# A channel attention with a rational feed-forward: second product with stationary weights, half of it in float32r

## The chip, the cores and the metric

The kernel runs on one core of a Trainium2 chip. Its time is the device time of one execution in microseconds (us). Five engines work side by side, each through its own list of instructions in order: TensorE (PE) for matrix products, with its weight loads shown apart (PEld), VectorE (DVE), ScalarE (ACT), GpSimd (POOL), and SyncE (SP), which issues the DMAs.

## The reference

```
B, N, C = 4, 6080, 256;  F = 2048
qn = q / (norm(q, axis=1) + 1e-6);  kn = k / (norm(k, axis=1) + 1e-6)
a  = softmax(kn^T @ qn / tau)            # 256 x 256 per batch
x  = (v @ a) as 24320 x 256
h  = x @ w_in                            # 24320 x 2048
P  = a0 + a1 h + a2 h^2 + a3 h^3
Q  = 1 + |b0| |h| + |b1| h^2
g  = P / (Q + 1e-6)
out = g @ w_out                          # 24320 x 256
```

All in float32. The attention is small; the two products with w_in and w_out and the rational function between them, on 24320 x 2048 elements, are nearly all the work.

## The kernel before

The attention matrix of a batch is multiplied into w_in once ("fuse"), so that h of a batch is v times a fused 256 x 2048 weight. These weights and v are each split into a high part in float32r and a low rest in float32r.

Work goes in groups of 512 tokens, twelve to a batch, 48 in all; the last group of each batch has 448. A group is worked on in eight **pairs**; a pair is two blocks of 128 columns of h (`pair`, line 612). For one pair:

- `mm1` (625): the first product. For each of the two blocks six matmuls with 512 columns (high by high, high by low, low by high, for two blocks of 128 input channels) into `hx`, two PSUM banks.
- The denominator: in the plain form ScalarE squares h, GpSimd multiplies and adds one ("line"), ScalarE takes b0|h|, GpSimd adds ("sum", a two-tensor operation). In the factored form (|h| (b1|h| + b0)), for the pairs in `FACTORED` = 1, 3, 6 of all groups but the first, ScalarE, VectorE ("prod"), ScalarE make it, and GpSimd only adds one ("one").
- The numerator: ScalarE ("slope") and two operations of VectorE ("num1", "num2"), in place in `hx`.
- The quotient: ScalarE takes the reciprocal square root of the denominator and squares it ("root", "square": r), GpSimd multiplies the denominator by r ("again": d r, close to 1), VectorE multiplies the numerator by r ("quot"), and then by 2 - d r ("last", a Newton step), into `g`. All these work on both blocks at once, 128 x 1024 elements.
- `mm2` (679): the second product in float32. A block of g of 128 tokens is the stationary side and 256 columns of w_out move; four tokens blocks for each of two column blocks, summed over all pairs into `acc`, two PSUM banks.

PSUM has eight banks: three `hx` of two banks, one `acc` of two. After its eight pairs, `finish` (691) copies `acc` with ScalarE into `orow` and SyncE stores it. The v of the next group comes through `values` (586): eight turns on TensorE, a copy on ScalarE, a subtraction on VectorE ("vlo").

The order of all instructions is written out beforehand by a planner (`Planner`, 68). Every step has an engine, a cost, a key and the buffers that it reads and writes. The planner plays the engines forward with these costs; an engine that is free takes the ready step with the lowest key whose buffers are free. Keys are the pair's place in the sequence plus an offset by kind of step (`LAG`, `TIME`, 21 to 30). The order found is then issued as it is: each engine keeps to it. A buffer's slot is given back when its last reader is done.

The first 120 us hold the attention of batch 0, and the preparation of w_in and w_out (`piece`, 304), which arrive as 64-bit floats and are turned into float32 by six operations a piece, mostly on VectorE. The attention of the next batches is worked on beside the pairs.

Of the kernel before, what the change touches and what calls it, by code (L numbers as in the profile page):

```python
# [21 lines left out]
    "first": 1.66, "prod": -1.1, "abs": -4.14, "line": 6.02, "second": 2.32, "sum": -18.3, "slope": 3.87,  # L22
    "num1": 23.26, "num2": 17.29, "root": 6.75, "one": -11.27, "square": -9.08, "again": 5.6, "quot": 15.77,
    "last": 10.51, "out": 27.17,
}
TIME = {
    "pair": 4.08, "start": 48.71, "load": 1.95, "softmax": 50.67, "in": 4.96, "late_in": 4.46, "out0": 2.34,
    "out": 5.84, "attn0_0": -0.36, "attn_0": 0.78, "attn0": 3.79, "attn": 2.32, "attn1": 91.81,
    "value": 3.37, "fuse": 1.73, "finish": 7.89, "front": 48.7, "front_pace": 3.02,
}  # L30

# [18 lines left out]
class Buf:  # L50


    def __init__(self, tag=None, view=None):
        self.tag, self.view = tag, view
        self.tile, self.slot = None, None
        self.writers, self.readers = [], []
        self.left = 0
        self.owner, self.until = None, 0.0
# [4 lines left out]

class Step:
    __slots__ = ("eng", "cost", "fn", "key", "need", "after", "new", "bufs", "banks", "port", "n")


class Planner:
# [3 lines left out]

    HOP = {"PE": 0.25, "ACT": 0.07, "DVE": 0.07, "POOL": 0.07, "SP": 3.5}

    def __init__(self, slots, fifo, banks):
        self.slots, self.fifo, self.banks = slots, fifo, banks
        self.steps = []

    def add(self, eng, cost, key, fn, reads=(), writes=(), port=False):
        s = Step()  # L80
        s.eng, s.cost, s.fn, s.key = eng, cost, fn, key
        s.n = len(self.steps)
        s.port = port or eng == "POOL"
        s.after, s.new, s.bufs = [], [], []
        before = {}
        for b in reads:
            for w in b.writers:
                before[w.n] = w
            assert b.writers
# [21 lines left out]
    def order(self):  # L111
# [5 lines left out]
        for q in queue.values():  # L117
            q.sort(key=lambda s: (s.key, s.n), reverse=True)
# [9 lines left out]
        left = len(self.steps)  # L128

        def fits(s):  # L130
            want = {}
            for b in s.new:
                want[b.tag] = want.get(b.tag, 0) + 1
                if b.tag in queue and queue[b.tag][-1] is not s:
                    return False
            if any(b.owner != s.eng and b.until > now for b in s.banks):
                return False
            return all(len(free[t]) >= n for t, n in want.items())

        while left:  # L140
            for e in ready:
                while busy[e] <= now and ready[e]:
                    skipped, pick = [], None
                    while ready[e]:
                        entry = heapq.heappop(ready[e])
# [8 lines left out]
                    for b in pick.new:  # L154
                        b.slot = free[b.tag].pop(0)
                        if b.tag in queue:
                            queue[b.tag].pop()
                    out.append((now, pick))
                    left -= 1
                    busy[e] = now + pick.cost  # L160
                    if pick.port:
                        other = "POOL" if e == "DVE" else "DVE"
                        busy[e] = max(now, port[other]) + pick.cost
                        port[e] = busy[e]
                    for b in pick.banks:
                        b.owner, b.until = e, busy[e] + self.HOP[e]
                    heapq.heappush(events, (busy[e], 0, pick.n, pick))
                    heapq.heappush(events, (busy[e] + self.HOP[e], 1, pick.n, pick))
# [4 lines left out]
            while events and events[0][0] <= now:  # L173
                _, what, _, s = heapq.heappop(events)
                if what == 2:
# [16 lines left out]
def tile_channel_attention_rational_ffn(  # L192
# [25 lines left out]
    while n0 < N:  # L218
# [8 lines left out]
    FACTORED = (1, 3, 6)  # L227

# [10 lines left out]
    SLOTS = {"hx": 3, "acc": 1, "d": 4, "uu": 4, "r": 3, "g": 4, "w": 10, "kq": 4, "sq": 2, "ssq": 1,  # L239
             "vst": 1, "vhi": 2, "vlo": 2, "orow": 2, "sacc": 1, "eT": 1, "cv": 1, "cv2": 1, "n2": 1,  # L240
             "s0": 1, "y": 1, "e": 1, "rn": 1, "diag": 1, "row": 1, "ex": 2, "sm": 2, "st": 1}
    plan = Planner(SLOTS, ("d", "uu", "r", "g", "w", "kq", "sq", "cv", "cv2", "vst", "vhi", "vlo", "orow", "acc"), ("hx", "acc"))

# [22 lines left out]
    def step(eng, cost, key, fn, reads=(), writes=(), port=False):  # L266
        new = [b for b in writes if b.tag is not None and not b.writers]
# [6 lines left out]
        plan.add(eng, cost, key, run, reads, writes, port)  # L274
# [20 lines left out]
    w_out_sb = const.tile([P, NF, C], F32, name="w_out_sb")  # L295
# [8 lines left out]
    def piece(side, m, at, c):  # L304
# [9 lines left out]
        raw = buf("d" if early else "g", [P, 2 * PIECE], U32, "raw")  # L314
        kept = buf("uu" if early else "cv", [P, 2, PIECE], F32, "kept")
        work = buf(("acc" if side == "in" and m < 4 else "hx") if early else "cv2", [P, 2, PIECE], F32, "work")
# [39 lines left out]
        def cut_off():  # L356
# [3 lines left out]
                dst, keep(), 1.125 * 2.0**-15, unit(F32), op0=ALU.is_ge, op1=ALU.mult  # L360
            )

        if side == "in":
            dst, ok = w_in_sb[:, j, cols], w_in_ok[part, j]
        else:
            dst, ok = w_out_sb[:, 2 * m : 2 * m + 2].rearrange("p f e -> p (f e)"), w_out_ok[m]
# [8 lines left out]
        step("DVE", two, c + 0.5, cut_off, [work, kept], [ok], port)  # L375


    class Attn:
# [3 lines left out]
        def __init__(self, b, begin, pace, end, gate=()):  # L382
# [3 lines left out]
            sps = buf("hx", [P, 2, GT], F32, "sps") if first else None  # L386
            self.sacc = None if first else buf("sacc", [P, 512], F32)
            self.front = FRONT if b == 1 else 0
            if self.front:
                sps = buf("acc", [P, 2, GT], F32, "fronts")  # L390
# [9 lines left out]
        def half(self, i, at, both, sps):  # L400
# [16 lines left out]
            if first or i < self.front:  # L417
                fn = lambda: self.products(sps, [kq], pn, i == 0, i == (self.front or 2 * NG) - 1)
                step("PE", 1.75, both, fn, [kq, sps] if i else [kq], [sps])
                if i == self.front - 1:  # L420
                    fn = lambda: dve.tensor_copy(self.sacc.tile, sps[:, 0, :])
                    step("DVE", 0.66, both + 1, fn, [sps], [self.sacc])
            elif half == 1:
                pair, slot = list(self.kq), buf("hx", [P, 2, GT], F32, "sps")
                step("PE", 3.5, both, lambda: self.products(slot, pair, pn, True, True), pair, [slot])
                if i == 1:
                    fn = lambda: dve.tensor_copy(self.sacc.tile, slot[:, 0, :])
                    step("DVE", 0.66, both + 1, fn, [slot], [self.sacc])
                else:
                    fn = lambda: dve.tensor_tensor(self.sacc.tile, slot[:, 0, :], self.sacc.tile, op=ALU.add)  # L430
# [13 lines left out]
        def products(self, slot, halves, pn, first, last):  # L444
            todo = [(x, t, c) for x in halves for t in range(T // 2) for c in range(NC2)]
            for n, (x, t, c) in enumerate(todo):
                pe.matmul(
                    slot[:, 0, c * C : (c + 1) * C], x[:pn, t, 0, c * P : (c + 1) * P], x[:pn, t, 1, :],
# [3 lines left out]
        def softmax(self, at):  # L452
            b = self.b
            W = 2 * NC2
            nps = buf("hx", [P, 2, GT], F32, "norms")
            n2, s0, y, e, rn = (buf(t, [P, W], F32) for t in ("n2", "s0", "y", "e", "rn"))
            diag, row = buf("diag", [P, NC2, P], F32), buf("row", [P, C], F32)
# [31 lines left out]
            def spread():  # L489
                for i in range(NC2):  # L490
                    dve.tensor_scalar_mul(diag[:, i, :], ident, rn[:, NC2 + i : NC2 + i + 1])

            step("DVE", 0.5, at + 0.05, spread, [rn], [diag], True)

            def rows():
                for i in range(NC2):
                    pe.matmul(
                        nps[:, 1, i * P : (i + 1) * P], ones, diag[:, i, :],
# [3 lines left out]
            step("PE", 0.8, at + 0.06, rows, [diag, nps], [nps])  # L502
            step("ACT", 0.45, at + 0.07, lambda: act.copy(row.tile, nps[:, 1, :C]), [nps], [row])
            sn = [buf("sq", [P, C], F32, f"sn{i}") for i in range(NC2)]
            ex = [buf("ex", [P, C], F32, f"ex{i}") for i in range(NC2)]
            low = [buf("sm", [P, 4], F32, f"low{i}") for i in range(NC2)]
            stat = buf("st", [P, 2 * NC2], F32, "stat")

            def scores(i):

                s = self.scores[:, 0] if b == 0 else self.scores.tile
                dve.scalar_tensor_tensor(
                    sn[i].tile, s[:, i * C : (i + 1) * C], rn[:, i : i + 1], row.tile,
                    op0=ALU.mult, op1=ALU.mult,
                )
                dve.tensor_reduce(low[i][:, 0:1], sn[i].tile, axis=AX.X, op=ALU.min)
# [243 lines left out]
```

## Time and profile before

| what | value |
|---|---|
| median of three runs | 2681.49 us (2680.3 to 2681.88) |
| span of the profiled execution, first to last instruction | 2678.6 us |
| TensorE busy, share of the span | 2647.2 us, 99% |
| weight loads | 2269.0 us, 85% |
| VectorE | 2219.5 us, 83% |
| ScalarE | 2198.0 us, 82% |
| GpSimd | 2105.4 us, 79% |
| mean granted clock of TensorE | 0.998 |
| moved by DMA | 110.10 MB, 41 GB/s |

How to read the rows: L43 is the line of a helper that issues every instruction, so groups are told apart by the names of the buffers: `acc<-w_out_sb,g` is the second product, `hx<-vhi,w` and `hx<-vlo,w` the first, `d<-d,r` on POOL the step "again", `g<-d,hx` on DVE the step "last", `hx<-hx,coef,r` "quot", `hx<-uu,coef,hx` "num2", `uu<-uu,hx` "num1", `d<-uu,babs,hx` "prod". A row of a group ends with busy us, mean ns of one, and after the second bar the idle time of the engine ahead of it. A float32 matmul is two records in the trace, a float32r matmul one.

### The profile page before, as it was taken

Reading aid. Unit: us, or ns where it says so; the run is one execution under the profiler, and the core shown is the slowest. Engines: PE = TensorE matmul, PEld = TensorE weight load, DVE = VectorE, ACT = ScalarE, POOL = GpSimd, SP = SyncE. Lnnn points to the kernel's source line nnn. Section 1 sums busy time; section 2 is a strip of 40 time slices with the busy share of each in tenths; the row PEclk is TensorE's granted clock in tenths of the full one; section 3 lists DMA queues with packets and bytes.
Section 4 is the critical chain, followed back from the end, with each engine's and each line's share of the span. In section 5 each row is a group of like instructions: output and inputs, shape, how many; then the busy total and the mean of one; then the engine's idle time right before and its main releaser. Section 6 shows DMA issues by size and latency. Waiting matters only on the chain.

```text
span 2678.6 us, 32541 instructions
## 1 busy us (share of the span) xinstructions
PE 2647.2 (99%) x12224; PEld 2269.0 (85%) x12224; DVE 2219.5 (83%) x1992; ACT 2198.0 (82%) x2231; POOL 2105.4 (79%) x1104
## 2 busy tenths in 40 slices
PE   7999999999999999999999999999999999999999
PEld 6788888888888888888888888888888888888887
DVE  7987888888787778888878877878887888888886
ACT  5787888888888887888878887878887888888885
POOL 6898778778678888877868888877875787787785
PEclk9999999999999999999999999999999999999999
DMA  9421000000011111110001121100000000000000
GB/s 335 126 63 62 16 32 17 17 31 16 17 31 55 56 48 52 42 32 31 17 16 47 45 66 48 46 17 32 16 16 16 31 16 17 32 16 17 31 9 15
DMA packets 69325, 110.10 MB, mean 41 GB/s; under 512 B 5296, under 2 KB 53936, under 8 KB 69168
## 3 DMA queue, kind: packets, MB, share of 16 engines
q1 hardware_dynamic: 69168, 108.03, 12.1%
q8 instruction: 96, 1.57, 0.2%
q14 instruction: 61, 0.50, 0.1%
HBM read 83.10 MB, written 24.90 MB: 40 GB/s over the span
## 4 chain that ended last, share of the span: by engine, by line
PE 89%; POOL 5%; ACT 2%; DVE 2%; issue 1%; DMA 1%; SPq 0%; DVEq 0%; ACTq 0%; POOLq 0%
PE acc L43 47%; PE hx L43 43%; POOL d L43 3%; POOL ssq L43 1%; DVE hx L43 1%; POOL orow L43 1%; ACT uu L43 1%; ACT r L43 0%; ACT L43 0%; DVE uu L43 0%; ACT d L43 0%; DVE g L43 0%; DMA r<-in_q_dram 0%; DVE orow L43 0%; DMA kq<-in_q_dram 0%
## 5 line engine op out<-in xcount | busy, mean ns | idle before, releaser
L43 PE MATMUL acc<-w_out_sb,g 128*128 128x256 f32 (+1 forms) x6144 | 1371.6, 379 | 0.7 <-DVE sacc L43 0.7
L43 PEld LDWEIGHTS acc<-w_out_sb,g 128*128 128x128 f32 (+1 forms) x6144 | 1155.6, 189 | 167.9 <-DVE sacc L43 0.9
L43 POOL TENSOR_TENSOR d<-d,r 128x1024 f32<-128x1024 f32 (+1 forms) x384 | 905.9, 2362 | 185.2 <-ACT r L43 172.1
L43 PE MATMUL hx<-vhi,w 128*128 128x512 f32 (+1 forms) x3072 | 1019.9, 401 | 5.7 <-DVE g L43 2.5
L43 PEld LDWEIGHTS hx<-vhi,w 128*128 128x128 f32 x3072 | 577.1, 188 | 122.8 <-DVE g L43 3.0
L43 DVE TENSOR_TENSOR uu<-uu,hx 128x1024 f32<-128x1024 f32 (+1 forms) x384 | 462.5, 1205 | 198.0 <-ACT uu L43 197.0
L43 PE MATMUL hx<-vlo,w 128*128 128x512 f32 (+1 forms) x1536 | 595.5, 388 | 0.0
L43 POOL TENSOR_TENSOR d<-d,uu 128x1024 f32<-128x1024 f32 (+1 forms) x243 | 573.8, 2361 | 20.3
L43 DVE SCALAR_TENSOR_TENSOR hx<-hx,coef,r 128x1024 f32<-128x1024 f32 (+1 forms) x384 | 490.4, 1279 | 109.8 <-ACT r L43 93.6
L43 DVE SCALAR_TENSOR_TENSOR g<-d,hx 128x1024 f32<-128x1024 f32 (+1 forms) x384 | 463.5, 1207 | 57.8 <-PE acc L43 20.5
L43 DVE SCALAR_TENSOR_TENSOR hx<-uu,coef,hx 128x1024 f32<-128x1024 f32 (+1 forms) x384 | 489.7, 1275 | 8.0
L43 ACT ACTIVATE r<-d 128x1024 f32<-128x1024 f32 (+1 forms) x384 | 404.2, 1053 | 74.9 <-POOL d L43 68.9
L43 ACT ACTIVATE uu<-hx,babs 128x1024 f32<-128x1024 f32 (+1 forms) x384 | 424.3, 1105 | 47.3 <-PE hx L43 47.3
L43 ACT ACTIVATE uu<-hx,coef 128x1024 f32<-128x1024 f32 (+1 forms) x384 | 458.4, 1194 | 0.0
L43 ACT ACTIVATE r<-r 128x1024 f32<-128x1024 f32 (+1 forms) x384 | 403.3, 1050 | 12.2
L43 ACT ACTIVATE d<-hx 128x1024 f32<-128x1024 f32 (+1 forms) x243 | 246.9, 1016 | 167.7 <-PE hx L43 167.4
L43 POOL TENSOR_SCALAR d<-d,babs 128x1024 f32<-128x1024 f32 (+1 forms) x243 | 271.7, 1118 | 141.5 <-ACT d L43 140.9
L43 PEld LDWEIGHTS hx<-vlo,w 128*128 128x128 f32 x1536 | 289.0, 188 | 54.9
L43 POOL TENSOR_SCALAR d<-d,ones 128x1024 f32<-128x1024 f32 (+1 forms) x141 | 157.3, 1116 | 146.4 <-ACT r L43 146.4
L43 ACT ACTIVATE d<-d 128x1024 f32<-128x1024 f32 (+1 forms) x141 | 146.6, 1040 | 64.6 <-DVE d L43 64.5
L43 POOL TENSOR_TENSOR ssq<-sq,ssq 128x1024 f32<-128x1024 f32 (+1 forms) x69 | 166.1, 2407 | 41.8 <-ACT sq L43 40.2
L43 DVE SCALAR_TENSOR_TENSOR d<-uu,babs,hx 128x1024 f32<-128x1024 f32 (+1 forms) x141 | 178.1, 1263 | 16.3 <-ACT uu L43 16.3
(84 smaller groups left out, 1063.5 us busy)
## 6 DMA issues: line engine op xcount, KB each, us to landing
vst<-in_v_dram SPq DMA_DIRECT2D x44, 512.0 KB, 3.5
out_dram<-orow SPq DMA_DIRECT2D x44, 512.0 KB, 2.6
kq<-in_k_dram SPq DMA_DIRECT2D x78, 256.0 KB, 3.6
kq<-in_q_dram SPq DMA_DIRECT2D x78, 256.0 KB, 3.9
d<-in_moe_w_in_dram SPq DMA_DIRECT2D x8, 512.0 KB, 6.6
r<-in_k_dram SPq DMA_DIRECT2D x10, 256.0 KB, 6.5
r<-in_q_dram SPq DMA_DIRECT2D x10, 256.0 KB, 6.4
d<-in_moe_w_out_dram SPq DMA_DIRECT2D x4, 512.0 KB, 7.1
```

The costliest lines, as they stand in the source:

```text
L43: ins = op(*args, **kwargs)
```

## The change

The second product has the weights of w_out as its stationary side and up to 512 tokens of g as its columns. The sums of a group so lie with output channels on the partitions; `finish` copies them to SBUF with ScalarE, turns them back with eight transposes on TensorE into the same two banks of `acc`, copies them again with ScalarE, and stores them.

Four of the eight pairs (0, 2, 4, 6; "R") run the second product in float32r. For them w_out is split into a high and a low part when it is prepared (two more operations a piece), and g too: the high part is quot itself, n r; the low part is (n - d n r) r, where "again" on GpSimd makes d n r, "rest" on VectorE subtracts, and GpSimd multiplies by r ("last_pool"). Three products are summed: high weights by high g, low weights by high g, high weights by low g. The other four ("S") stay in float32 as before. All steps from "quot" on are issued for each block of 128 x 512 by itself.

Six of the eight pairs (0, 2, 3, 4, 6, 7) have the factored denominator, in every group.

An `hx` is now two buffers, `hA` and `hB`, one per bank, taken together but given back one by one; the two halves of `mm1` are steps of their own, and small users take one bank. `d` has three slots instead of four, the fused weights nine instead of ten, `g` is kept by halves (six for high, four for low parts, four for S). The late pieces of w_out use `uu` and `d` instead of buffers of their own, the softmax uses two `kq` slots. The planner has a separate offset for every step and pair, counts an engine as free a little before its step ends, and can hold back steps far ahead.

```diff
+KIND = ("RFP", "SU", "RFP", "SF", "RFP", "SU", "RFP", "SF")
...
+class Pair:
+    def __init__(self, low, high):
+        self.low, self.high = low, high
+        high.mate, low.leads = low, True
...
-    SLOTS = {"hx": 3, "acc": 1, "d": 4, "uu": 4, "r": 3, "g": 4, "w": 10, "kq": 4, "sq": 2, "ssq": 1,
+    SLOTS = {"hA": 3, "hB": 3, "acc": 1, "d": 3, "uu": 4, "r": 3, "gh": 6, "gl": 4, "g": 4, "w": 9, "kq": 4, "sq": 2, "ssq": 1,
...
+    def banks(view=None):
+        def whole(slot):
+            t = homes["hx"][slot].rearrange("p (a b) -> p a b", a=2)
+            return t if view is None else view(t)
+        return Pair(Buf("hA", whole), Buf("hB", whole))
...
+        def low_part():
+            dve.tensor_tensor(wlo, top(F32), whi.bitcast(F32), op=ALU.subtract)
...
+        step("ACT", 0.6, c + 0.6, lambda: act.activation(whi, top(F32), AF.Copy), [work], [part])
+        step("DVE", two, c + 0.7, low_part, [work, part], [ok], port)
...
+        for i in range(2):
+            step("PE", 1.38 * s, at + 0.01 * i, lambda i=i: mm1(i), [whi, wlo, vhi, vlo], [hx.both[i]])
+
+        def mm2(i, w, x, first, last):
+            for a, g in zip(w, x):
                 for e in range(NC2):
+                    pe.matmul(
+                        acc[:, e, :n], a[:, W_AT[p] + i, e * P : (e + 1) * P], g[:, :n],
+                        start=(first and a is w[0]), stop=(last and a is w[-1]),
+                    )
...
+        def quot(i, out):
+            dve.scalar_tensor_tensor(out, hx[:, i, :n], a0, r[:, i, :n], op0=ALU.add, op1=ALU.mult)
+
+        def rest(i, out):
+            dve.scalar_tensor_tensor(out, hx[:, i, :n], a0, d[:, i, :n], op0=ALU.add, op1=ALU.subtract)
...
         for i in range(2):
...
+            if kind[0] == "S":
+                g = buf("g", [P, GT])
+                fn = lambda i=i: pool.tensor_tensor(d[:, i, :n], d[:, i, :n], r[:, i, :n], op=ALU.mult)
...
+                fn = lambda i=i, g=g, end=end, old=old: mm2(i, (w_out_sb,), (g,), not old, end)
...
+            ghi, glo = buf("gh", [P, GT], F32R), buf("gl", [P, GT], F32R)
+            step("DVE", cost(0.53, 0.2), key + LAG["quot"][p], lambda i=i, g=ghi: quot(i, g[:, :n]), [h, r], [ghi], rank=at + 10.0)
+            fn = lambda i=i, g=ghi: pool.tensor_tensor(d[:, i, :n], d[:, i, :n], g[:, :n].bitcast(F32), op=ALU.mult)
...
+                step("DVE", cost(0.53, 0.2), key + LAG["rest"][p], lambda i=i: rest(i, d[:, i, :n]), [h, d, t], [left])
+                fn = lambda i=i, g=glo: pool.tensor_tensor(g[:, :n], d[:, i, :n], r[:, i, :n], op=ALU.mult)
...
+            fn = lambda i=i, g=ghi, old=old: mm2(i, (w_out_hi, w_out_lo), (g, g), not old, False)
...
+            fn = lambda i=i, g=glo, end=end: mm2(i, (w_out_hi,), (g,), False, end)
...
     def finish(G, at, acc):
...
-        orow = buf("orow", [P, T, C])
-        step("ACT", 1.05, at, lambda: act.copy(orow[:pn], acc[:pn]), [acc], [orow])
+        turned, orow = buf("orow", [P, NC2, GT], F32, "oT"), buf("orow", [P, T, C])
...
+        step("ACT", 1.05, at, lambda: act.copy(turned[:, :, :n], acc[:, :, :n]), [acc], [turned])
+
+        def back():
+            for t in range(T):
+                for e in range(NC2):
+                    pe.transpose(
+                        natural()[:pn, t, e * P : (e + 1) * P], turned[:, e, t * pn : (t + 1) * pn], ident
+                    )
+
+        step("PE", 1.1, at + TIME["back"], back, [turned], [slot, orow])
+        step("ACT", 1.05, at + TIME["store"], lambda: act.copy(orow[:pn], natural()[:pn]), [slot], [orow])
```

More of the change, by code (lines that the diff above doesn't have):

```diff
@@ L21 @@
 LAG = {
-    "first": 1.66, "prod": -1.1, "abs": -4.14, "line": 6.02, "second": 2.32, "sum": -18.3, "slope": 3.87,
-    "num1": 23.26, "num2": 17.29, "root": 6.75, "one": -11.27, "square": -9.08, "again": 5.6, "quot": 15.77,
-    "last": 10.51, "out": 27.17,
+    "first": (-23.943, 0.779, 16.152, -2.628, 12.275, -14.299, 0.849, 12.204),
+    "second": (64.578, 55.323, 59.143, 56.607, 7.413, 49.338, 52.686, 69.362),
+    "line": (11.809, -44.33, -0.798, -23.493, 7.232, -28.691, -20.654, -32.78),
@@ L137, in fits, with take @@
                 return False
-            return all(len(free[t]) >= n for t, n in want.items())
+            low = None
+            for b in s.new:
+                if b.tag == "hA":
+                    low = b
+                elif b.tag == "hB" and b.mate is not None and b.mate is not low:
+                    if b.mate.slot not in free["hB"]:
+                        return False
+            if low is not None and any(b.mate is low for b in s.new) and not set(free["hA"]) & set(free["hB"]):
+                return False
+            return all(len(free[t]) >= n for t, n in want.items())
+        def take(b):
+            spare = free[b.tag]
+            if b.tag == "hA":
+                other = set(free["hB"])
+                good = [x for x in spare if (x in other) == b.leads]
+                slot = min(good or spare)
+            elif b.tag == "hB":
+                if b.mate is not None:
+                    slot = b.mate.slot
+                else:
+                    other = set(free["hA"])
+                    slot = min([x for x in spare if x not in other] or spare)
+            else:
+                slot = spare[0]
+            spare.remove(slot)
+            return slot
         while left:
@@ L313, in piece @@
         early = (side, m) in EARLY
-        raw = buf("d" if early else "g", [P, 2 * PIECE], U32, "raw")
-        kept = buf("uu" if early else "cv", [P, 2, PIECE], F32, "kept")
-        work = buf(("acc" if side == "in" and m < 4 else "hx") if early else "cv2", [P, 2, PIECE], F32, "work")
+        raw = buf("d" if early else "uu", [P, 2 * PIECE], U32, "raw")
+        kept = buf("uu", [P, 2, PIECE], F32, "kept")
+        if not early or (side == "in" and m < 4):
+            work = buf("acc" if early else "d", [P, 2, PIECE], F32, "work")
+        else:
+            work = banks()
         port = not early
@@ L374, in piece @@
         step("DVE", two, c + 0.4, together, [work, kept], [work], port)
-        step("DVE", two, c + 0.5, cut_off, [work, kept], [ok], port)
+        if dst is not None:
+            step("DVE", two, c + 0.5, cut_off, [work, kept], [ok], port)
+            return
+        part = Buf()
+        step("DVE", two, c + 0.5, cut_off, [work, kept], [work], port)
+        step("ACT", 0.6, c + 0.6, lambda: act.activation(whi, top(F32), AF.Copy), [work], [part])
+        step("DVE", two, c + 0.7, low_part, [work, part], [ok], port)
     class Attn:
@@ L672, in pair @@
-        fn = lambda: dve.scalar_tensor_tensor(c(hx), c(hx), a0, c(r), op0=ALU.add, op1=ALU.mult)
-        step("DVE", 1.28 * s, at + LAG["quot"], fn, [hx, r], [hx])
-        fn = lambda: dve.scalar_tensor_tensor(
-            c(g), c(d), 2.0, c(hx), op0=ALU.subtract, op1=ALU.mult, reverse0=True
-        )
-        step("DVE", 1.28 * s, at + LAG["last"], fn, [d, hx], [g])
-        def mm2(i):
-            for t in range(T):
-                pe.matmul(
-                    acc[:pn, t, :], g[:, i, t * pn : (t + 1) * pn], w_out_sb[:, 2 * p + i, :],
-                    start=(p == 0 and i == 0 and t % 2 == 0), stop=(p == NFP - 1 and i == 1),
-                    skip_group_check=True,
-                )
```

296 lines of the change are left out of this document (195 added, 101 removed).

## The prediction

> **What bounds the kernel now.** I read the page first: its engine line and the shares of the chain that ended last.
>
> ```profile
> span 2678.6 us, 32541 instructions
> ...
> PE 2647.2 (99%) x12224; PEld 2269.0 (85%) x12224; DVE 2219.5 (83%) x1992; ACT 2198.0 (82%) x2231; POOL 2105.4 (79%) x1104
> ...
> PE 89%; POOL 5%; ACT 2%; DVE 2%; issue 1%; DMA 1%; SPq 0%; DVEq 0%; ACTq 0%; POOLq 0%
> ```
>
> TensorE owns the chain. A busy matmul row can hide slack, because matmuls overlap, so the next two views are the waits of TensorE between 120 and 2600 us, and the busy time before, in and after that stretch (columns: PE, PEld, DVE, ACT, POOL, clock, DMA share, GB/s).
>
> ```profile
> PE hx L43 <- DVE g L43: 1.3, 2, 0.9
> PE hx L43 <- DVE w_out_sb L43: 1.2, 1, 1.2
> PE hx L43 <- DVE w L43: 0.7, 4, 0.2
> PE hx L43 <- DVE sacc L43: 0.5, 1, 0.5
> ...
> 0.00:120.00 120.00, 99.11 (x435) 83.54 (x436) 100.07 (x134) 78.18 (x97) 82.37 (x43) 0.96 0.73 245
> 120.00:2600.00 2480.00, 2475.98 (x11454) 2123.50 (x11453) 2067.05 (x1813) 2071.31 (x2084) 1975.96 (x1035) 1.00 0.10 32
> 2600.00:2678.60 78.60, 72.15 (x339) 61.91 (x337) 52.35 (x47) 48.55 (x52) 47.10 (x27) 0.99 0.04 13
> ```
>
> From 120 to 2600 us TensorE waits 3.7 us in all, at a granted clock of 1.00, while VectorE is 83% busy. What an instruction less on TensorE is worth there is its spacing, as long as no other engine fills up. The chain in order of time gives the spacings, over one change of group:
>
> ```profile
> 335.39 8.63 PE acc L43 x40
> 344.02 0.87 PE hx L43 x8
> 344.89 1.73 PE acc L43 x8
> 346.62 8.21 PE hx L43 x36
> 354.83 8.63 PE acc L43 x40
> ...
> 2613.38 2.44 PE hx L43 x12
> ...
> 2650.96 22.46 PE acc L43 x104
> ...
> 2673.45 1.01 ACT orow L43
> ```
>
> A record of the second product (128 weights, 256 columns, float32, two records to a matmul) takes 8.63/40 = 0.2158 us. A float32r matmul of the first product with 512 columns takes 8.21/36 = 0.228 us, with 448 columns (the short last group of a batch) 2.44/12 = 0.203 us. A turn of a 128x128 float32 block takes 0.87/8 = 0.109 us. And between the last second product of one group and the first of the next TensorE has 8.2 us of first products to do.
>
> **TensorE, part by part.** Per group of 512 tokens the second product is now 8 pairs x 16 records x 0.2158 = 27.62 us. Afterwards four pairs (S) stay in float32 with the weights stationary: 4 matmuls of 512 columns a pair. No such record is in the trace. [...] I take 13.81 us for the four, at the upper end. The other four (R) run 12 float32r matmuls each: three products (high weights by high g, low weights by high g, high weights by low g), two halves, two output blocks. Same type and shape as the first product: 4 x 12 x 0.228 = 10.94 us. Saved: 27.62 - 24.75 = 2.87 us. Added: eight turns, 0.87 us. Net 2.00 us a group, 88 us over the 44 full groups. In the four short groups the second product costs the same now (22.46/104 = 0.216), because the tokens are the stationary side; afterwards they are the columns: S 13.81 x 448/512 = 12.08, R 48 x 0.203 = 9.74, turns 0.87, net 4.9 us, 20 us in all. TensorE loses **108 us** of work.
>
> The row for the float32r spacing is 0.228 us. [...]
>
> **The ends.** After the last second product there come two handoffs, eight turns and a second copy: 0.87 + 1.01 + about 0.3 = +2.2 us. In the front, two early R pieces of w_out add one VectorE operation each, two late ones another; these read SBUF twice and may be slow beside GpSimd:
>
> ```profile
> L43 DVE SCALAR_TENSOR_TENSOR w_out_sb<-cv,cv 128x512 f32<-128x512 f32 x4 | 7.5, 1872 | 0.0
> L43 DVE SCALAR_TENSOR_TENSOR w_out_sb<-uu,hx 128x512 f32<-128x512 f32 x4 | 2.8, 689 | 0.3
> ```
>
> That is 2 x 0.69 + 2 x 1.87 = 5.1 us, on an engine that is busy 100 of the first 120 us, so I count all of it (bounds 0 and, if the late pieces also hold back pairs by the d and uu buffers they now borrow, 15). ScalarE's four copies there (0.6 us) lie beside it. Floor of TensorE: 2678.6 - 108 + 2.2 + 5.1 = **2578 us** of span.
>
> **VectorE, the engine that fills.** Its groups by shape, and four of its instructions in a row:
>
> ```profile
> L43 DVE SCALAR_TENSOR_TENSOR hx<-hx,coef,r 128x1024 f32<-128x1024 f32 x352 | 453.7, 1290 | 100.0 <-ACT r L43 85.1 <-DVE hx L43 0.5 <-ACT uu L43 0.5
> L43 DVE SCALAR_TENSOR_TENSOR hx<-uu,coef,hx 128x1024 f32<-128x1024 f32 x352 | 452.8, 1286 | 7.2
> L43 DVE SCALAR_TENSOR_TENSOR hx<-uu,coef,hx 128x896 f32<-128x896 f32 x32 | 36.9, 1154 | 0.9
> L43 DVE SCALAR_TENSOR_TENSOR g<-d,hx 128x1024 f32<-128x1024 f32 x352 | 428.7, 1218 | 47.8 <-POOL d L43 15.9 <-PE acc L43 13.2 <-PE hx L43 0.5
> L43 DVE SCALAR_TENSOR_TENSOR g<-d,hx 128x896 f32<-128x896 f32 x32 | 34.7, 1085 | 10.0 <-PE acc L43 7.3 <-POOL d L43 1.3 <-issue 1.0
> L43 DVE TENSOR_TENSOR uu<-uu,hx 128x1024 f32<-128x1024 f32 x352 | 427.9, 1216 | 181.5 <-ACT uu L43 180.9
> L43 DVE SCALAR_TENSOR_TENSOR d<-uu,babs,hx 128x1024 f32<-128x1024 f32 x129 | 164.4, 1274 | 16.3 <-ACT uu L43 16.3
> L43 DVE TENSOR_TENSOR vlo<-hx,vhi 128x1024 fp32r<-128x1024 f32 x44 | 53.6, 1218 | 0.8 <-ACT vhi L43 0.6
> L43 DVE SCALAR_TENSOR_TENSOR w<-hx,st,w 128x256 fp32r<-128x256 f32 x64 | 27.8, 477 | 23.3 <-ACT w L43 23.2
> L43 DVE TENSOR_TENSOR sacc<-hx,sacc 128x512 f32<-128x512 f32 x28 | 19.2, 686 | 8.6 <-PE hx L43 8.6
> ...
> 1000.16 1.21 DVE L43 TENSOR_TENSOR uu<-uu,hx 128x1024 f32<-128x1024 f32 x1
> 1001.29 1.27 DVE L43 SCALAR_TENSOR_TENSOR d<-uu,babs,hx 128x1024 f32<-128x1024 f32 x1
> 1002.50 1.22 DVE L43 SCALAR_TENSOR_TENSOR g<-d,hx 128x1024 f32<-128x1024 f32 x1
> 1003.64 1.28 DVE L43 SCALAR_TENSOR_TENSOR hx<-uu,coef,hx 128x1024 f32<-128x1024 f32 x1
> ```
>
> Packed instructions start about 0.08 us before the one ahead ends, so I charge durations less 0.08. Now a pair costs 1.14 + 1.21 + 1.21 + 1.14 = 4.69 us, and with the factored denominator (three of eight) 1.19 more: 41.1 us a group. A half of 512: from 1286 and 1154 ns an element costs 1.03 ns, so a half with a coefficient is 1286 - 528 = 758 ns, and from 1218 and 1085 the last one is 686 ns; charged 0.68 and 0.61. Afterwards R has four halves with a coefficient (quot, rest; its last product goes to GpSimd), S two and two; six of eight pairs are factored. R: 2.34 + 1.19 + 2.71 = 6.25; S unfactored 2.34 + 2.57 = 4.91; S factored 6.10. A group: 25.0 + 9.8 + 12.2 = **47.0 us, 5.9 more**. Over 44 groups and four at 0.885 that is 2235 us, with vlo, w and sacc 105 more: 2340 us behind the front. At TensorE's floor there are 2578 - 125 = 2453 us for it: VectorE must be packed to 95%. Today's mean in the long stretch is 83%. So some of the 108 us will not come.
>
> **GpSimd and ScalarE.**
>
> ```profile
> L43 POOL TENSOR_TENSOR d<-d,r 128x1024 f32<-128x1024 f32 x352 | 838.8, 2385 | 148.2 <-ACT r L43 136.1 <-POOL d L43 1.2
> L43 POOL TENSOR_TENSOR d<-d,uu 128x1024 f32<-128x1024 f32 x223 | 531.7, 2384 | 18.6
> L43 POOL TENSOR_TENSOR d<-d,r 128x896 f32<-128x896 f32 x32 | 67.2, 2101 | 37.0 <-ACT r L43 36.0
> L43 POOL TENSOR_SCALAR d<-d,babs 128x1024 f32<-128x1024 f32 x223 | 251.4, 1127 | 103.3 <-ACT d L43 102.7
> L43 POOL TENSOR_SCALAR d<-d,ones 128x1024 f32<-128x1024 f32 x129 | 145.1, 1125 | 130.2 <-ACT r L43 130.2
> L43 ACT COPY orow<-acc 128x1024 f32<-128x1024 f32 x44 | 44.6, 1014 | 34.4 <-PE acc L43 29.5 <-DMA vst<-in_v_dram 4.9
> ```
>
> GpSimd: 147 pairs more are factored (288 against 141), each 1.13 + 2.38 - 1.13 = 2.38 us less: -350. The last product of 192 R pairs, 2.385 each: +458. Splitting: a fixed part of 2385 - 1024 x 2.22 = 113 ns (2.22 ns from the 1024 and 896 rows), 576 times: +65. Sum 2278 us, 88% of 2600. ScalarE: 48 second copies, 49 us, to 2250 us. Neither binds by itself, but both are later more often.
>
> **The forecast.** I take VectorE at 94%, between today's mean and the 95% of the floor, nearer to the latter because VectorE can take its next instruction from any of three pairs in flight: 125 + 2340/0.94 = 2614, and some 6 us at the end when only TensorE and the copies work: 2620 of span. The median of the runs shown is 2681.49, 2.9 above the profiled span; so **2623 us**. Its own range is 2597 to 2650 (VectorE at 95% to 93%).
>
> **The rivals.** *TensorE stays packed.* The three PSUM pairs, now freed by bank, keep it fed and VectorE really reaches 95%: 2578 + 3 = 2581. For it: 3.7 us of waits today. Against it: four engines at 99, 95, 88 and 86%.
>
> *VectorE binds below 93%.* A chain through an R pair alternates VectorE and GpSimd four times (quot, again, rest, last), and an instruction that needs its forerunner's result can't use the overlap. At 92% it is 125 + 2543 + 6 + 3 = 2677, no change; at 91% 2705. [...]
>
> *The turnaround of the only acc, slower than before.* A group's sums are copied out (1.01), turned in the same two banks (0.87), copied again (1.01), with three handoffs about 3.3 us, and the next group's second product waits for all of it, behind it in TensorE's order. Today one copy sits under 8.2 us of first products, which needs all three PSUM pairs free at that moment. If VectorE, fuller, has none free, the 3.3 us are idle: 48 x 3.3 = 158, 2581 + 158 = 2739. It decides from 2.1 us idle a group (100/48).
>
> *The change doesn't do what it says*: the split R product runs at the float32 spacing, 48 x (0.4316 - 0.228) = 9.8 us a group more, above 3000. The first product's rows speak against it.
>
> **How the numbers follow.** Forecast 0.50; TensorE packed 0.17; VectorE below 93% 0.20 (of it faster 0.09, same 0.05, slower 0.06); turnaround 0.12; no gain in rate 0.01. Faster by over 0.2% (what a measurement of this kernel can tell): 0.50 + 0.17 + 0.09 = 0.76. Within 0.2%: 0.05. Slower: 0.06 + 0.12 + 0.01 = 0.19. The range runs from 2572 (the packed case less the 4 us of the S records and 5 of the front) to 2700 (VectorE near 91%); it leaves out the turnaround, the rate and the worst of VectorE, about 0.16.
>
> **What would show it.** R matmuls of the second product spaced 0.228 us, S records 0.43, eight turns in 0.87. TensorE's waits between 120 and 2550 us of 30 to 60 us in total, released by VectorE's g and hx rather than by ScalarE's copy of acc. VectorE at 93 to 96%, GpSimd near 88%. A wait on the second copy of acc near 3 us, 48 times, would prove the turnaround; waits below 15 us the packed case. I am wrong in the working if halves on VectorE take far from 0.76 and 0.69 us.

## The result, and the profile after

The changed kernel takes 2873.49 us (median of four runs, 2872.46 to 2874.18) where the kernel before takes 2681.68 on the same chip: ratio **1.0716** (95% interval 1.0701 to 1.0731). It is 192 us slower; 2623 was forecast.

The page of the changed kernel, its span, engines and the chain that ended last:

```profile
span 2871.1 us, 30342 instructions
...
PE 2642.3 (92%) x10304; PEld 1858.2 (65%) x10304; DVE 2480.3 (86%) x2911; ACT 2246.2 (78%) x2285; POOL 2290.1 (80%) x1725
...
PE 48%; DVE 33%; issue 6%; POOL 6%; ACT 5%; DMA 0%; DVEq 0%; SPq 0%; POOLq 0%; ACTq 0%
```

No engine is full (the granted clock of TensorE was 1.00 from 120 to 2800 us, as in the kernel before, so the clock is not the reason). TensorE has fallen from 99 to 92%, and in the chain it now alternates with VectorE, 48 and 33%, where it had 89%. The waits between 130 and 2800 us (engine and what it writes, what it waits for; us in all, times, longest):

```profile
ACT uu L64 <- PE hx L64: 264.5, 180, 6.2
POOL d L64 <- DVE gh L64: 257.0, 141, 4.5
...
PE hx L64 <- DVE d L64: 79.7, 92, 1.4
DVE g L64 <- PE hx L64: 77.4, 70, 1.8
DVE d L64 <- PE hx L64: 75.1, 62, 4.2
PE hx L64 <- DVE g L64: 73.3, 87, 3.7
```

The last four rows are the finding. TensorE's first product waits for VectorE's `d` ("rest") and `g` ("last"): that is the wait for a free PSUM bank. But `d` and `g` also wait for the first product, 152 us in 132 waits, though what each reads from its bank is a result that VectorE itself wrote there ("num2", "quot") after TensorE had done with that bank. In the kernel before, the row of `g<-d,hx` put 0.5 us of its idle time down to the first product. The instructions in order of time (start, duration, idle time before in brackets) show what they wait for, and the prices of the new operations:

```profile
454.65 0.63 PE L64 MATMUL acc<-gh,w_out_lo 128*128 128x512 f32 x2
455.12 0.62 PE L64 MATMUL acc<-gl,w_out_hi 128*128 128x512 f32 x2
455.58 1.03 PE L64 MATMUL hx<-ident,vst 128*128 128x128 f32 x8
456.45 3.60 PE L64 MATMUL acc<-g,w_out_sb 128*128 128x512 f32 x8
...
662.62 3.59 PE L64 MATMUL acc<-g,w_out_sb 128*128 128x512 f32 x8
666.05 1.04 PE L64 MATMUL hx<-ident,vst 128*128 128x128 f32 x8
...
1213.49 0.39 PE L64 MATMUL hx<-vhi,w 128*128 128x512 f32 x1
...
1214.63 0.39 PE L64 MATMUL hx<-vhi,w 128*128 128x512 f32 x1
...
1215.12 0.75 DVE L64 SCALAR_TENSOR_TENSOR d<-hx,coef,d 128x512 f32<-128x512 f32 x1 [1.08 <-PE hx L64]
...
1215.93 0.19 PEld L64 LDWEIGHTS hx<-vhi,w 128*128 128x128 f32 x1 [1.33 <-DVE d L64]
1215.93 0.50 PE L64 MATMUL hx<-vhi,w 128*128 128x512 f32 x1 [0.91 <-DVE d L64]
```

By the planned order TensorE, from 1213.49 on, writes the first bank of a tile for a new pair. The last matmul ends at 1214.63 + 0.39 = 1215.02. Only then, 0.1 us later, does VectorE start "rest", which reads the *second* bank for the old pair: 1.08 us idle. And only when "rest" has ended (1215.87) does TensorE start on the second bank, 0.91 us idle. The planned order reckoned with both at once.

### The profile page after: what moved, and what is told of

Same layout as the page of the kernel before. It is cut to its first block, busy times and chain, and to the rows that moved or that the text cites. A ratio compares the mean times of both kernels' runs of the same rounds, so it can differ in the third digit from the quotient of the medians.

```text
span 2871.1 us, 30342 instructions
## 1 busy us (share of the span) xinstructions
PE 2642.3 (92%) x10304; PEld 1858.2 (65%) x10304; DVE 2480.3 (86%) x2911; ACT 2246.2 (78%) x2285; POOL 2290.1 (80%) x1725
## 4 chain that ended last, share of the span: by engine, by line
PE 48%; DVE 33%; issue 6%; POOL 6%; ACT 5%; DMA 0%; DVEq 0%; SPq 0%; POOLq 0%; ACTq 0%
PE hx L64 31%; PE acc L64 17%; DVE hx L64 12%; DVE d L64 7%; DVE uu L64 6%; DVE g L64 5%; POOL d L64 4%; DVE gh L64 3%; ACT uu L64 2%; ACT r L64 1%; ACT d L64 1%; POOL gl L64 1%; POOL ssq L64 1%; POOL orow L64 1%; ACT sq L64 0%
## 5 line engine op out<-in xcount | busy, mean ns | idle before, releaser
L64 POOL TENSOR_TENSOR d<-d,gh 128x512 f32<-128x512 f32 (+1 forms) x384 | 484.1, 1281 | 267.4 <-DVE gh L64 266.9
L64 PE MATMUL acc<-g,w_out_sb 128*128 128x512 f32 (+1 forms) x1536 | 688.9, 587 | 1.1 <-DVE g L64 1.1
L64 POOL TENSOR_TENSOR gl<-d,r 128x512 fp32r<-128x512 f32 (+1 forms) x384 | 489.3, 1281 | 74.5 <-DVE d L64 70.9
L64 POOL TENSOR_TENSOR d<-d,r 128x512 f32<-128x512 f32 (+1 forms) x384 | 480.8, 1273 | 39.4 <-ACT r L64 36.5
L64 PEld LDWEIGHTS acc<-g,w_out_sb 128*128 128x128 f32 x1536 | 289.9, 189 | 273.2 <-issue 254.9
L64 DVE SCALAR_TENSOR_TENSOR d<-uu,babs,hx 128x1024 f32<-128x1024 f32 (+1 forms) x288 | 364.1, 1264 | 45.8 <-ACT uu L64 42.3
L64 DVE SCALAR_TENSOR_TENSOR d<-hx,coef,d 128x512 f32<-128x512 f32 (+1 forms) x384 | 282.7, 741 | 123.8 <-PE hx L64 79.5
L64 DVE SCALAR_TENSOR_TENSOR g<-d,hx 128x512 f32<-128x512 f32 (+1 forms) x384 | 256.9, 679 | 99.8 <-PE hx L64 78.4
L64 DVE SCALAR_TENSOR_TENSOR hx<-hx,coef,r 128x512 f32<-128x512 f32 (+1 forms) x384 | 288.2, 751 | 22.6 <-ACT r L64 12.9
L64 DVE SCALAR_TENSOR_TENSOR gh<-hx,coef,r 128x512 fp32r<-128x512 f32 (+1 forms) x384 | 269.3, 740 | 25.3 <-ACT r L64 15.0
```

Of the source, the lines that this page charges most:

```text
L64: ins = op(*args, **kwargs)
```

## The experiments

Two theories stood at the start. **Tile:** the two banks of an `hx` tile are ordered as one thing between engines, so a bank that is given back by itself gains nothing and adds a wait in the other direction. **VectorE and GpSimd:** VectorE's greater load, or its handovers with GpSimd in the R pairs, set the time and the banks are beside the point. A third was the prediction's turnaround of `acc`. "Before" had medians of 2680.1 to 2681.8 us beside these runs. Rows without a ratio are kernels that leave out a part of the computation; each of them was run once.

| kernel | what differs from the changed one | us | ratio to before (95%) |
|---|---|---|---|
| split | a PSUM tile per bank | 2705.69 | 1.0096 (1.0079 to 1.0113) |
| joint | banks of a tile given back together | 2792.49 | 1.0411 (1.0394 to 1.0429) |
| flip | the tie between the banks turned round | 2856.05 | 1.0649 (1.0631 to 1.0666) |
| nonum1 | VectorE's num1 left out | 2799.11 | |
| split_nonum1 | a PSUM tile per bank, and num1 left out | 2652.01 | |
| noback | no turning back | 2869.48 | |
| joint_noback | joint, no turning back | 2796.80 | |
| nolow | no low part of g | 2680.95 | |
| turn_only | before, and only the stationary side changed | 2724.08 | 1.0161 (1.0144 to 1.0178) |

**One bank against the other (banks).** A kernel of its own: 100 turns, first with two halves of one tile, then with two tiles of one bank each.

```
            pe.matmul(where, x[:, :P], x, start=(n == 0), stop=(n == 5))
...
            products(left)
            dve.scalar_tensor_tensor(y, right, 0.5, raw, op0=ALU.add, op1=ALU.subtract)
...
    phase(both[:, :512], both[:, 512:])
    phase(one, two)
```

In each turn `products(left)` writes six matmuls into one bank, and VectorE reads the other (`right`), which was written once before the turns began. The first phase uses the two banks of one tile, the second two tiles of one bank each.

> Leaves out the whole computation: 100 turns of six float32r matmuls of 512 columns into one PSUM bank while VectorE reads another bank (one operation of 128 x 512), first with both banks in one tile, then with each bank a tile of its own. Tile theory (a tile of two banks is ordered as one thing between TensorE and the other engines): in the first part the two engines take turns, 6 x 0.228 + 0.75 + about 0.2 for two handoffs = 2.3 us a turn, 230 us; in the second they overlap, 1.37 us a turn, 137 us. If instead the banks themselves can't be used by two engines at once, both parts take about 230 us; if neither, both take 137 us.

It took 401.29 us as a whole, its stores included. The groups by shape, and the order of time in each phase:

```profile
L31 PE MATMUL both<-x 128*128 128x512 f32 x606 | 167.9, 413 | 81.8 <-DVE y L31 77.7 <-ACT x L31 4.2
L31 PE MATMUL one<-x 128*128 128x512 f32 x600 | 136.2, 389 | 0.0
...
L31 DVE SCALAR_TENSOR_TENSOR y<-both,raw 128x512 f32<-128x512 f32 x100 | 69.2, 692 | 181.3 <-PE both L31 181.3
L31 DVE SCALAR_TENSOR_TENSOR y<-two,raw 128x512 f32<-128x512 f32 x100 | 69.1, 691 | 4.0 <-PE two L31 0.7
```

```profile
59.80 0.69 DVE L31 SCALAR_TENSOR_TENSOR y<-both,raw 128x512 f32<-128x512 f32 x1 [1.76 <-PE both L31]
...
60.55 1.66 PE L31 MATMUL both<-x 128*128 128x512 f32 x6 [0.78 <-DVE y L31]
62.24 0.69 DVE L31 SCALAR_TENSOR_TENSOR y<-both,raw 128x512 f32<-128x512 f32 x1 [1.75 <-PE both L31]
...
299.71 4.47 PE L31 MATMUL one<-x 128*128 128x512 f32 x19
299.76 4.32 DVE L31 SCALAR_TENSOR_TENSOR y<-two,raw 128x512 f32<-128x512 f32 x6
```

With one tile the two engines take strict turns, 62.24 - 59.80 = 2.44 us a turn. With two tiles TensorE never waits, 136.2/100 = 1.36 us a turn, and VectorE waits 4.0 us in all. So here it is not the PSUM that can't serve both; it is the tile.

**A tile for each bank in the kernel itself (split).** The order on each engine is the changed kernel's, and nothing is left out; an instruction of ScalarE or VectorE that reads or writes both banks becomes two, one for each.

```diff
-            t = homes["hx"][slot].rearrange("p (a b) -> p a b", a=2)
-            return t if view is None else view(t)
+            return Two(homes["hA"][slot], homes["hB"][slot])
...
-        fn = lambda: dve.tensor_tensor(c(y), c(y), c(hx), op=ALU.mult)
+        fn = lambda: [dve.tensor_tensor(y[:, i, :n], y[:, i, :n], hx[:, i, :n], op=ALU.mult) for i in range(2)]
```

> Each pair of feed-forward tiles gets two PSUM tiles of one bank in place of one tile of two banks, so that nothing ties the one bank to the other. Instructions that read or wrote both banks are made in two halves (ScalarE's 'first', 'second' and 'slope', VectorE's 'prod', 'num1', 'num2', the copies of v); steps and their order on each engine stay the changed kernel's, nothing is left out. The price, from the changed kernel's rows: VectorE 2 x 679 - 1207 = 151 ns more for each of 384 num1, 2 x 751 - 1279 = 223 ns for each of 384 num2 and 288 prod, some 215 us in all on top of 2480, so VectorE cannot end below about 2695; ScalarE gets some 900 instructions more. Theory (the two-bank tile, ordered as one between engines, makes VectorE and TensorE wait for each other): faster than the changed kernel's 2873 all the same, 2760 to 2840, with VectorE busy 95% or more, no wait of VectorE for a matmul into the bank it doesn't read, and TensorE's idle time before mm1 mostly for VectorE being busy. Rival (VectorE's work and the handover between VectorE and GpSimd set the time, the tile is beside the point): slower than 2873 by most of the 215 us, 2950 to 3080.

Measured 2705.69, 168 us less than the changed kernel with more work on two engines. Its page, and all that VectorE waited for:

```profile
span 2703.3 us, 32576 instructions
...
PE 2599.8 (96%) x10304; PEld 1859.8 (69%) x10304; DVE 2538.5 (94%) x4015; ACT 2390.3 (88%) x3197; POOL 2289.3 (85%) x1725
...
DVE 52%; POOL 17%; ACT 13%; issue 10%; PE 8%; DMA 0%; SPq 0%; POOLq 0%; DVEq 0%; ACTq 0%
```

```profile
DVE d L64 <- POOL d L64: 57.9, 80, 2.8
DVE uu L64 <- ACT uu L64: 17.2, 14, 2.8
DVE gh L64 <- ACT r L64: 16.9, 13, 3.4
...
DVE sacc L64 <- PE hA L64: 0.4, 1, 0.4
```

The tile theory is borne out, even beyond its range: `d` and `g` wait for TensorE no more, VectorE goes from 86 to 94% busy and owns the chain. But split changes one thing more than the tie. A half can start as soon as its own bank is written, while TensorE still writes the other:

```profile
1295.69 0.60 ACT L64 ACTIVATE d<-hA 128x512 f32<-128x512 f32 x1 [0.86 <-PE hA L64]
...
1295.95 0.63 PE L64 MATMUL hB<-vhi,w 128*128 128x512 f32 x2
```

So the 168 us are for the untied banks and for this earlier start together; how they divide was not measured. I had priced the halves too high. VectorE grew by 58 us, not by 215, because I summed durations; but the next instruction starts 0.08 to 0.09 us before the one ahead has ended:

```profile
1301.46 0.68 DVE L64 TENSOR_TENSOR uu<-uu,hA 128x512 f32<-128x512 f32 x1
1302.05 0.68 DVE L64 TENSOR_TENSOR uu<-uu,hB 128x512 f32<-128x512 f32 x1
1302.65 0.75 DVE L64 SCALAR_TENSOR_TENSOR hA<-uu,coef,hA 128x512 f32<-128x512 f32 x1
```

Two halves of num1 take 1302.65 - 1301.46 = 1.19 us of VectorE, little more than the 1.14 us charged for one whole.

**VectorE relieved, with the tie and without (nonum1, split_nonum1).** num1 is left out of every pair, first in the changed kernel, then in split.

```diff
-        fn = lambda: dve.tensor_tensor(c(y), c(y), c(hx), op=ALU.mult)
+        fn = lambda: None
```

> The changed kernel in the same order without the VectorE operation num1 of every pair (the numerator is then a1 + a2 + a3 h instead of its square part): 384 operations of 1.21 us, 435 us or 18% of VectorE's work, left out. VectorE theory: the time follows VectorE, by 250 us or more, to 2620 or less. Tile theory: the waits between matmuls and readers stay, a link of 1.2 us of the chain falls away where it was the last, 2830 us, between 2790 and 2850. Turnaround theory: 2873 within 20.

> The same with VectorE's num1 left out of every pair, so that VectorE has room (2067 us of work in the changed kernel without num1, plus some 158 for the halves, 2225 in all); the comparison is with the changed kernel without num1, 2799 us. Left out of the computation: the product num1 of the numerator. Theory (two-bank tile): with VectorE no bound and no tie between the banks, TensorE's 2517 us of own work come within reach: 2600 to 2700, 100 to 200 below 2799 in spite of more instructions. Rival (handover between VectorE and GpSimd, whatever the tile): 2799 or slower, 2790 to 2880.

Measured 2799.11 and 2652.01. nonum1, its engines and two of its waits:

```profile
PE 2611.0 (93%) x10304; PEld 1856.1 (66%) x10304; DVE 2067.1 (74%) x2527; ACT 2244.3 (80%) x2285; POOL 2287.8 (82%) x1725
```

```profile
DVE g L64 <- PE hx L64: 131.6, 71, 2.4
DVE d L64 <- PE hx L64: 119.9, 63, 5.0
```

Taking 413 us of busy time from VectorE gave 74 us, and VectorE then waits 252 us for first products. That VectorE's load by itself sets the time is refuted. Untying the banks (with the halves' earlier start) is worth another 147 us on top, and 168 without the relief.

**Giving the banks back together (joint).** The same steps, but the two buffers of an `hx` come free only when both are done with, and single users take both; keys unchanged, order planned anew.

```diff
+                        if b.left:
+                            continue
+                        if b.partner is None:
                             free[b.tag].append(b.slot)
+                        elif not b.partner.left:
+                            free[b.tag].append(b.slot)
+                            free[b.partner.tag].append(b.partner.slot)
```

> The changed kernel, but the two banks of a tile are given back only when both are done with, and users of a single bank take both; nothing else differs, the order is planned again. Tile theory: the waits of VectorE on matmuls into the other bank (158 us in the changed kernel's profile) and most of those of TensorE on VectorE's d, g and hx behind them (169 us) go, though every bank is held longer: about 2720 us, between 2680 and 2780. VectorE theory (VectorE is too full to be packed with three pairs in flight): banks held longer can only hurt, 2873 or more. Turnaround theory (the only acc is missing while it is turned back): no change, 2873 within 20.

Measured 2792.49: 81 us better than the changed kernel, though 12 us above the range that I expected. VectorE's waits for `hx` are gone as such; in their place a pair holds both banks until its later half is done. Chain and one of the waits:

```profile
POOL 30%; PE 21%; ACT 19%; DVE 19%; issue 10%; DMA 1%; SPq 0%; POOLq 0%; DVEq 0%; ACTq 0%
```

```profile
PE acc L64 <- ACT orow L64: 70.0, 34, 2.7
...
PE hx L64 <- DVE g L64: 13.3, 15, 3.4
```

So a plan that knows the tie beats one that doesn't, but it recovers 81 us where split recovers 168. As the order was planned anew too, these 81 us are not the tie alone. The granted clock also differs: 0.981 to 0.983 on average in joint's runs, 0.993 in the changed kernel's. If all of the time followed the clock, that would hide some 31 us more (0.011 x 2792, an upper estimate).

**The tie turned round (flip).** In the changed kernel the program has TensorE's write to the free bank ahead of VectorE's read of the other, so VectorE waits. Here each engine keeps its order, but the write stands behind the read, so TensorE waits.

```diff
-    steps = plan.order()
+    steps = flipped(plan.order())
```

> The changed kernel with the same order of instructions on every engine. Only the order in which they are written down across engines differs: a matmul into one bank is written behind the last reader of the other bank of its tile, so that of two instructions on different banks the matmul waits for the reader and not the reader for the matmul. Tile theory: a reader takes 0.7 us and the matmuls 1.37, so turning about 150 such waits round saves up to 0.3 us each with what hangs on them, 2845 us, between 2820 and 2862. VectorE and turnaround theory: the order of work is the same, 2873 within 5.

Measured 2856.05, 17 us less, inside the tile theory's range where the other theories expected no change. VectorE's `d` and `g` wait for the first product no more, and TensorE waits instead, 175 us where it was 158 over the whole run:

```profile
PE hx L64 <- DVE g L64: 94.5, 83, 3.1
PE hx L64 <- DVE d L64: 80.3, 75, 3.3
```

The order in which instructions of different engines are written down decides who waits. So the tie lies in the waits that the program is built with. Who waits for whom matters little for the time.

**No turning back (noback, joint_noback).** The eight turns and the second copy of a group are left out, in the changed kernel and in joint; the output stays with channels on the partitions.

```diff
-            for t in range(T):
-                for e in range(NC2):
-                    pe.transpose(
...
+            pass
...
-        step("ACT", 1.05, at + TIME["store"], lambda: act.copy(orow[:pn], natural()[:pn]), [slot], [orow])
+        step("ACT", 1.05, at + TIME["store"], lambda: None, [slot], [orow])
```

> The changed kernel in the same order without the turning back: the eight transposes of a group and the second copy of acc are left out, and the sums are stored with output channels on the partitions. Turnaround theory: the time falls by the 158 us of the prediction's rival, to 2715. Tile theory: TensorE waited 1.7 us for copies of acc in the changed kernel's profile, so only the transposes go, and only where TensorE was the last: 2860, between 2830 and 2873.

> The same left out of the kernel whose banks are given back together (joint, 2792 us). There TensorE waits 70 us for copies of acc. If these are a bound of their own behind the waits between banks, the time falls by those 70 and up to 42 of transposes, to 2700, between 2680 and 2730; if the engines only wait for one another and would wait elsewhere, by less than 40, to 2760 or more.

Measured 2869.48 and 2796.80, -4 and +4 us; joint's own four runs spread over 8 us. The turnaround of `acc` is refuted as a cause, and joint's 70 us of waits for it are no bound: without them TensorE waits elsewhere, in joint_noback for "last", where joint had 13.3 us:

```profile
PE hx L64 <- DVE g L64: 67.2, 34, 3.4
```

So here 70 us of idle time of one engine were no price, where several wait in turns. (joint_noback's mean granted clock was 0.975, again lower, which may hide a part of a gain.)

**No low part (nolow).** "again", "rest" and "last_pool" are left out of the R pairs; the third product runs on the high part again, so that TensorE's work is unchanged.

```diff
-            fn = lambda i=i, g=ghi: pool.tensor_tensor(d[:, i, :n], d[:, i, :n], g[:, :n].bitcast(F32), op=ALU.mult)
+            fn = lambda: None
...
-            fn = lambda i=i, g=glo, end=end: mm2(i, (w_out_hi,), (g,), False, end)
+            fn = lambda i=i, g=ghi, end=end: mm2(i, (w_out_hi,), (g,), False, end)
```

> The changed kernel in the same order without the making of the low part of g in the four R pairs: again and last product on GpSimd and rest on VectorE are left out (1152 operations of 1.2 us on GpSimd less 384 that remain in S, and 384 of 0.66 on VectorE); the low product on TensorE runs with the high part in its place, so TensorE's work is the same. Tile theory: half of the waits between banks (those of rest) go and a bank of an R pair is given back after quot, some 4 us earlier: 2700, between 2640 and 2780. If the float32r pairs were not where the time is lost: 2820 or more.

Measured 2680.95, -192 us. The engines, and the tie that is left, in the S pairs:

```profile
PE 2592.5 (97%) x10304; PEld 1865.1 (70%) x10304; DVE 2244.8 (84%) x2527; ACT 2233.5 (83%) x2285; POOL 1338.5 (50%) x957
```

```profile
DVE g L64 <- PE hx L64: 62.0, 48, 2.1
```

Making the low part is thus a second condition of the loss. One way in which it can act is that the detour VectorE, GpSimd, VectorE keeps the bank until "rest" has run, so that a new pair is let into the neighbour bank in between; this is argued, not shown, because nolow also takes some 950 us of work from GpSimd and 235 from VectorE. VectorE's load is worth little here (nonum1); GpSimd's was not tested alone. Take away the low part and the kernel is where it was before; take away the tie and it nearly is. The two amounts, 192 and 168, cannot be added.

**Only the stationary side and the turning back (turn_only)**, added to the kernel before, all pairs in float32:

```diff
+                    acc[:, e, :n], w_out_sb[:, 2 * p + i, e * P : (e + 1) * P], g[:, i, :n],
...
+        step("PE", 1.1, at + 0.1, back, [turned], [slot, orow])
+        step("ACT", 1.05, at + 0.2, lambda: act.copy(orow[:pn], natural()[:pn]), [slot], [orow])
```

> The kernel before with one part of the change alone: weights stationary in the second product and sums turned back per group; everything else, also the pairs in one piece and the three pairs of banks, as before. Eight transposes of 0.109 us a group are 42 us, the four short groups save 14: 2710 if only TensorE's work counts. If the missing acc is felt with three pairs in flight (a first copy, transposes and a second copy, 3.3 us against 1.0), up to 48 x 2.3 = 110 us more, 2820.

Measured 2724.08, +44 us on the kernel before, and TensorE still owns the time:

```profile
PE 2676.3 (98%) x9536; PEld 1730.4 (64%) x9536; DVE 2226.7 (82%) x1992; ACT 2240.4 (82%) x2279; POOL 2107.0 (77%) x1104
...
PE 87%; ACT 4%; POOL 3%; DVE 3%; issue 2%; DMA 0%; SPq 0%; DVEq 0%; ACTq 0%; POOLq 0%
```

Turns add 42 us and the four short groups take off 14, so the expectation had TensorE's work 28 us up, and TensorE is busy 2676.3 - 2647.2 = 29 us longer. There the adding up comes out. The other 15 us are more idle time of TensorE: span less busy is 45.9 us here and was 31.4. So the turnaround of `acc` and all other new waits cost at most those 15 us here, where up to 110 were feared.

No kernel here that does all of the work beats the kernel before. The nearest, split, stays 0.96% behind it, with VectorE at 94%.

## Why the prediction was wrong, point by point

*TensorE's work: right.* In the timeline above two R matmuls take 455.12 - 454.65 = 0.47 and 455.58 - 455.12 = 0.46 us, 0.23 each (0.228 forecast); eight S records 666.05 - 662.62 = 3.43, 0.429 each (0.4316); eight turns 456.45 - 455.58 = 0.87 (0.87). Two terms of the forecast stand on no row of the kernel before. The 13.81 us for S took a record of 512 columns at twice the row's 0.2158 us, and the range allowed 4 us less for it: both were my estimates, and at 0.429 us the four pairs take 13.72 us a group, some 4 us less in all. The handoffs (about 0.3 us for two at the end, a third in the turnaround's 3.3) were an estimate too: at the end of the changed kernel the first copy, the turns and the second copy start 0.04, 0.05 and 0.04 us after what they wait for has ended. TensorE's busy time, 2642 us, hardly fell all the same. Waits lengthen it: a matmul that starts after one shows a longer record (0.50 us at 1215.93, 0.39 at 1214.63), and the same 10304 matmuls are 2567 us of busy time in split_nonum1. By the prediction's floor TensorE could have been done in 2578 us. It was let to work too late.

*VectorE's halves: right, its sum nearly.* The groups by shape:

```profile
L64 DVE SCALAR_TENSOR_TENSOR hx<-hx,coef,r 128x512 f32<-128x512 f32 x352 | 266.2, 756 | 20.8 <-ACT r L64 12.5 <-PE hx L64 0.6
L64 DVE SCALAR_TENSOR_TENSOR d<-hx,coef,d 128x512 f32<-128x512 f32 x352 | 261.2, 747 | 117.0 <-PE hx L64 75.9 <-POOL d L64 34.6 <-POOL gl L64 6.3
...
L64 DVE SCALAR_TENSOR_TENSOR g<-d,hx 128x512 f32<-128x512 f32 x352 | 237.5, 685 | 96.9 <-PE hx L64 78.4 <-POOL d L64 5.4 <-PE acc L64 2.1
```

756, 747 and 685 ns where 758 and 686 were worked out from whole operations. The sum behind the front was forecast as 2340 us and came to 2480 - 97 = 2383, 43 more; why was not taken apart. The same rows carry the waits: 75.9 and 78.4 us of idle time before them, for the first product.

*GpSimd and ScalarE: right.* 2290 us busy (2278 forecast) and 2246 (2250).

*The share: wrong, and this is the step that failed.* "I take VectorE at 94% ... because VectorE can take its next instruction from any of three pairs in flight." It can't: the order is fixed beforehand, and an instruction that waits holds up all behind it (VectorE does nothing in the 1.08 us ahead of "rest" in the timeline above). The windows of the changed kernel (columns as in the prediction) have it thus:

```profile
0.00:120.00 120.00, 94.27 (x394) 77.76 (x394) 97.22 (x151) 72.74 (x94) 66.92 (x37) 0.93 0.71 240
120.00:2800.00 2680.00, 2488.62 (x9672) 1737.70 (x9673) 2329.28 (x2695) 2127.48 (x2143) 2175.13 (x1648) 1.00 0.09 30
```

2329/2680 = 87%. The prediction's formula with the measured work and share gives 125 + 2383/0.869 + 9 = 2876, against 2873. That it comes out says little, since a share is nothing but work over time; but it splits the miss. With the measured work and the forecast 94% it gives 2669. So some 46 us of the miss of 250 are work that the sum lacked, and some 207 are the share. It also says that even at 94% the gain would have been about 12 us and not 59. I had let a share stand for the waits without asking what the *order of writes* to a tile would do. The diff said that a pair is given back bank by bank; I took it at its word ("now freed by bank", in the rival that went faster still) and asked only what it gains. Where the banks really are free one by one, in split, VectorE is busy for 94% of the span.

*The rivals.* TensorE packed (2581): out, its waits for VectorE's `d`, `g` and `hx` are not below 15 us; the first two alone make 153. VectorE below 93%: the figure went that way, to 87% and so past the 91% that it priced, and its alternation of VectorE and GpSimd in the R pairs may be part of the cause (nolow takes it away, with GpSimd's work), but VectorE's load by itself is not (nonum1). What this rival says of the overlap fits the kernel before: "quot" starts at 1005.03, 0.11 us after the "num2" ahead of it has ended (1003.64 + 1.28), where the three operations before that "num2" each end 0.06 to 0.08 us after the next has started. The turnaround (2739): the sign was right, the mechanism not (noback). The rate: R ran at the float32r spacing (0.23 us a matmul). None of them named the tie, and 2873 lay outside the range; the row to look at was in the diff, two halves of one PSUM tile handed to two engines at once.

*What would show it.* TensorE's waits between 120 and 2550 us were forecast at 30 to 60 us and came to 137 for `d` and `g` alone; they showed that the forecast had failed, but not why. The telling sign was in no list: waits in *both* directions between the same two engines on the same tile.

*Still open.* nolow, with TensorE's full new work, lies 101 us of span above TensorE's floor of 2578, split 125; how that divides between the tie that nolow keeps, VectorE's fill and the order, which was made for prices that no longer hold, was not taken apart. Nor was split's gain divided between the untied banks and the halves' earlier start, or nolow's between the bank held longer and GpSimd's work.

## What to carry to other kernels

Here a buffer came free at the grain at which its accesses are ordered, not at the grain at which the plan counted it: with two banks in one tile a turn took 2.44 us, with a tile for each 1.36. Before PSUM is handed over bank by bank, give each bank a tile of its own, or a planned overlap can turn into a wait in both directions (152 and 153 us in the changed kernel). Price a fuller engine by what it will wait for, not by a share: list, for the fullest buffer, who writes and who reads at the same time. And where the profile shows two engines waiting for each other on one name, ask which bytes each of them touches.

## What the runs showed that I had not expected

Matmuls into one bank and a VectorE read of another did not slow each other: 1.36 us a turn for six matmuls, 0.227 each where the prediction's row has 0.228, and 691 ns a read where it is 692 in strict turns. Two banks of one tile cost 2.44 us a turn. Splitting a VectorE operation of 1024 columns in two costs 0.05 us when its halves follow each other, not the 0.15 to 0.22 that their durations suggest. And leaving 413 us of work out of an 86% busy engine gave only 74.
